# Softmax of a decoding kernel with paired heads: the subtraction of the maxima on GpSimd, one exponential for both batches, the sums on VectorE, and one copy for a transposed activation

## The chip, the cores and the metric

The kernel runs on one core of one Trainium2 chip. The metric is the device time of one execution in microseconds. A profiled execution also leaves a trace, from which the profile page and all rows below come. Its span runs from the first to the last instruction; the device time contains the span and a little around it.

## The reference

One decoding step of a transformer block, in float32, for a batch of 2 and one new token each: the normalized input goes through attention over the last 2048 positions of a cache (32 heads of 128) and, in parallel, through a bilinear gated layer; both are added to the input.

```python
B, Sq, D = 2, 1, 512            # Hq = Hkv = 32, Sk = 8192, Dh = 128, F = 1376
W = min(4096, max(256, Sk // 4))                     # 2048 positions
xn = _layernorm(x, axis=-1)
q = (xn @ wq).reshape(B, Sq, Hq, Dh).transpose(0, 2, 1, 3)
k, v = k_cache[:, :, Sk - W:, :], v_cache[:, :, Sk - W:, :]
p = softmax(einsum("bhqd,bhkd->bhqk", q, k) * Dh ** -0.5)
A = einsum("bhqk,bhkd->bhqd", p, v).transpose(0, 2, 1, 3).reshape(B, Sq, Hq * Dh) @ wo
h = (xn @ w_gate) * (xn @ w_up)
return x + A + h @ w_down
```

Nearly all the bytes are the keys and values: 2 batches x 32 heads x 2048 positions x 128 x 4 bytes, twice.

## The kernel before, in words

**The stream.** All inputs but a small tail are laid out in one array in the order in which they are used, and come in as large transfers, all issued by SyncE. `blocks()` writes that order out by hand: a small first load (`first`: the input, two selection matrices and a piece of wq), then loads of up to 31 blocks of 512 elements per partition (7936 KB), and smaller ones at the end. A field is the keys of a head (`k`, 8 blocks, both batches), its values (`v`, 8 blocks), a slice of wq (1 block), a slice of wo (1 block), or a piece of the gated layer's weights. The values run three heads behind the keys (`LAG = 3`). The `steps` pool has three buffers. `pump()` issues the next load as soon as one is free, and `done()` counts the fields of a buffer down and calls `pump()` when the last one was used. So a buffer is given back by VectorE (after the sums over a head's keys) or by TensorE (after the values and wo), whichever comes last.

**Order.** `InOrder` keeps the instructions of TensorE, VectorE, ScalarE and SyncE in program order; waits between engines come from the tiles that they share. GpSimd's instructions stand outside of it, on their own queue. `groups()` cuts the work by units (keys or values of a head): after the first heads, groups alternate between two heads of keys with one of values (keys 4 and 5 with values 1; 7 and 8 with 4; and so on) and one head of keys with two of values (6 with 2 and 3; 9 with 5 and 6). The main loop runs these groups through head 27 (`EARLY`); heads 28 to 31 are written out by hand behind it, with filler matmuls (`keep_busy`) in between.

**One head.** `products(h)` multiplies, in place, the keys by q (128 x 4096 elements on VectorE; q stands in PSUM, spread over all partitions by `project_q`). `sums(h)` reduces each product over the 128 elements of the head: 32 scores per partition, 16 for each batch. `maxima(h)` takes the maximum per partition on VectorE and across partitions on GpSimd (`mm`). `weights(h)` turns it into a negative bias on ScalarE (`nm`), and takes one exponential for each batch, 16 elements each, whose accumulated sums go to `rs`; GpSimd adds these across the partitions (`sum`), and `reciprocals(h)`, one head later, inverts them on VectorE (`rec`). The weights land in a ring of six tiles `p` which is zero elsewhere, in the columns that `side(h)` gives (1 for every third head, else 0); as TensorE's stationary operand a slice of 16 columns of it gives both batches and two sides their own rows of the result. `values` multiplies the values by them (`weigh`), copies the result out (ScalarE), transposes it (`transpose`), scales each column by `rec` into `oT` (ScalarE), and projects by wo into `acc`.

**The gate.** After head 3, `gate()` multiplies the two halves of the gated layer and transposes the product by matmuls into `tr`; after each of four of these ScalarE copies six columns into `hT`; pieces of the remainder go to `hX`. `down` then multiplies by w_down.

**The end.** The last weighings, projections and w_down pieces follow the last loads; two halves of the output are added up and stored by SyncE and ScalarE.

Of the kernel before, what the change touches and what calls it, by code (L numbers as in the profile page):

```python
# [8 lines left out]
F32 = mybir.dt.float32  # L9
AF = mybir.ActivationFunctionType  # L10
ALU = mybir.AluOpType
AX = mybir.AxisListType
# [4 lines left out]
P = 128  # L17
B, D, H, DH, SK, F = 2, 512, 32, 128, 8192, 1376
W = min(4096, max(256, SK // 4))
J = W // P  # L20
NC = D // P
FB = 4 * P
NFB = -(-F // FB)
# [10 lines left out]
JG = J // 4  # L34
# [10 lines left out]
OWN = 4  # L45
TG = [(0, 8, OWN), (8 * OWN, FT - 8 * OWN, 1)]
TP = FT
PADS = 480, 376


def k(h):
# [28 lines left out]
def groups():  # L80

    units = [u for h in range(LAG, H - 1) for u in (("k", h), ("v", h - LAG))]
    parts = [[("k", 0), ("k", 1)], [("k", 2)], units[:2]]
    parts += [units[i : i + 3] for i in range(2, len(units), 3)]
    return [[[i for kind, i in p if kind == want] for want in "kv"] for p in parts]
# [61 lines left out]
def kernel(  # L147
# [8 lines left out]
    nc = tc.nc  # L156
    pe, dve, act, sp = (InOrder(tc, e) for e in (nc.tensor, nc.vector, nc.scalar, nc.sync))
    SCALE = float(DH) ** -0.5
    BUFS = 3

    const = ctx.enter_context(tc.tile_pool(name="const", bufs=1))
    steps = ctx.enter_context(tc.tile_pool(name="steps", bufs=BUFS))
    small = ctx.enter_context(tc.tile_pool(name="small", bufs=6))
# [3 lines left out]

    const.tile([P, PADS[0]], F32, name="pad0")
    wd_tail = const.tile([TP, D], F32, name="wd_tail")

    todo, at = [], 0
# [31 lines left out]
    def done(kind, i):  # L203
        nonlocal held
        _, key = got.pop((kind, i))
        left[key] -= 1
        if left[key] == 0 and key[0] != "f":
            del tiles[key]
            held -= 1
            pump()  # L210
# [21 lines left out]
    o_ps = [ps_c.tile([P, 4 * DH], F32, name=f"o_ps{i}") for i in range(2)]  # L232
# [2 lines left out]
    gu_ps = o_ps  # L235

    NP = 6
    p_ring = [const.tile([P, B, JG, 8 * B], F32, name=f"p{i}") for i in range(NP)]
    for t in p_ring:
        nc.gpsimd.memset(t, 0.0)  # L240


    oT_ring = [const.tile([P, M], F32, name=f"oT{i}") for i in range(4)]
# [2 lines left out]
    tr = ps_c.tile([P, 4 * P], F32, name="tr")  # L246
# [20 lines left out]
        xnb, xn.rearrange("p c b -> p (c b)").unsqueeze(2).to_broadcast([P, NC * B, P])  # L267
    )

    q_ps, s_t, mm_t, p_t, sum_t, rec_t, oT = {}, {}, {}, {}, {}, {}, {}  # L270
    n_acc = bank = 0

    def side(h):

        return int(h % 3 == 0)
# [3 lines left out]
    def project_first(i):  # L279
        w = got["w", i][0].rearrange("p (c n) -> p c n", c=NC)  # L280
        if i == 0:
            q = q_first
        else:
            q_ps[0] = ps_q.tile([P, B, GC], F32, name="q")
            q = q_ps[0][:, :, DH:]
        for b in range(B):
            for c in range(NC):
                pe.matmul(
                    q[:, b, :], xnb[:, c * B + b, :], w[:, c, :],
                    start=(c == 0), stop=(c == NC - 1),  # L290
                )
        done("w", i)

    def project_q(h):

        if h + HG >= H:
            return
        g, c = h // HG + 1, h % HG
        if c == 0:
            q_ps[g] = ps_q.tile([P, B, GC], F32, name="q")  # L300
        for b in range(B):
            pe.matmul(
                q_ps[g][:, b, :], xnb[:, c * B + b, :], got["wq", h][0],
                start=(c == 0), stop=(c == NC - 1),
            )
        done("wq", h)

    def k_of(h):
        return got["k", h][0].rearrange("p (b j d) -> p b j d", b=B, j=J)

    def products(h):
        g, hh = divmod(h, HG)
        kt = k_of(h)
        qb = q_ps[g][:, :, hh * DH : (hh + 1) * DH] if h else q_first
        dve.tensor_tensor(
            kt, kt, qb.unsqueeze(2).to_broadcast([P, B, J, DH]), op=ALU.mult
        )

    def sums(h):
        s_t[h] = small.tile([P, B, J], F32, name="s")  # L320
        dve.tensor_reduce(s_t[h], k_of(h), axis=AX.X, op=ALU.add)
        done("k", h)

    def maxima(h):
        s = s_t[h]
        m = small.tile([P, B], F32, name="m")
        dve.tensor_reduce(m, s, axis=AX.X, op=ALU.max)
        mm = small.tile([P, B], F32, name="mm")
        nc.gpsimd.partition_all_reduce(mm, m, P, bass_isa.ReduceOp.max)  # L329
        mm_t[h] = mm  # L330

    def weights(h):
        s, mm = s_t.pop(h), mm_t.pop(h)
        nm = small.tile([P, B], F32, name="nm")
        act.mul(nm, mm, -SCALE)
        p_t[h] = p_ring[h % NP]
        rs = small.tile([P, B], F32, name="rs")
        for b in range(B):
            act.activation(
                p_t[h][:, b, :, 8 * side(h) + 4 * b : 8 * side(h) + 4 * b + 4],  # L340
                s[:, b, :].rearrange("p (i r) -> p i r", r=4),
                AF.Exp, bias=nm[:, b : b + 1], scale=SCALE, accum_out=rs[:, b : b + 1],
            )
        sum_t[h] = small.tile([P, B], F32, name="sum")
        nc.gpsimd.partition_all_reduce(sum_t[h], rs, P, bass_isa.ReduceOp.add)  # L345

    def reciprocals(h):
        rec_t[h] = small.tile([P, B], F32, name="rec")
        dve.reciprocal(rec_t[h], sum_t.pop(h))
# [13 lines left out]
    def weigh(h, v, parts, first, last):  # L363

        for n, part in enumerate(parts):
            b, i = divmod(part, JG)
            pe.matmul(
                o_ps[bank][32 * i : 32 * i + 8 * B, :], p_t[h][:, b, i, :],
                v[:, FB * n : FB * (n + 1)], start=first and b == 0, stop=last and b == B - 1,
            )  # L370

# [45 lines left out]
    def values(heads):  # L417
        transpose(heads, pv(heads))
        for h in heads:
            project_o(h)  # L420


    hT = const.tile([P, 4, NFB, M], F32, name="hT")
# [18 lines left out]
    def gate():  # L442
        g_sb = small.tile([P, FB], F32, name="o_sb", bufs=2)
        act.copy(g_sb, gu_ps[0])
        h_sb = small.tile([P, FB], F32, name="o_sb", bufs=2)
        dve.tensor_tensor(h_sb, g_sb, gu_ps[1], op=ALU.mult)
        for i in range(4):
            t = tr[:, P + i * P // 2 : P + i * P // 2 + NFB * B]
            pe.matmul(t, h_sb[:, i * P : (i + 1) * P], rows, start=True, stop=True)
            act.copy(hT[:, i, :, :], t.rearrange("p (n b) -> p n b", b=B))  # L450
        f = (NFC % 4) * P
        own = slice((NFB - 1) * B, NFB * B)
        for i in range(2):
            t = tr[HP * i : HP * i + RX, P + P // 4 : P + P // 4 + NFB * B]
            pe.matmul(t, h_sb[:, f - M : f + FX], rows, start=True, stop=True)
            act.copy(hX[HP * i : HP * i + RX, i, :], t[:, own])
            one = rows[HP * i : HP * i + M, 2 * i * B : 2 * i * B + B]
            act.copy(hX[HP * i : HP * i + M, i, :], one)
        f += FX
        t = tr[:TP, P + 3 * P // 4 : P + 3 * P // 4 + NFB * B]  # L460
        pe.matmul(t, h_sb[:, f : f + TP], rows, start=True, stop=True)
        act.copy(hX[:TP, 2, :], t[:, own])
# [35 lines left out]
    spare_in = xnb.rearrange("p a b -> p (a b)")  # L498
    for i in range(2):
        project_first(i)  # L500
    for ks, vs in groups()[:-2]:
        for n, h in enumerate(ks):
            products(h)
            project_q(h)
            if 2 <= h <= 3:
                project_gu(h - 2)
            sums(h)
            if h == LAG:
                gate()
            if vs and n == 0 and h < EARLY:  # L510
                values(vs)
            if h == LAG:
                down(0)
                down_rest()
            maxima(h)
            weights(h)
            if h >= 1:
                reciprocals(h - 1)
            if h == EARLY:
                values(vs)  # L520

# [2 lines left out]
        keep_busy(GC)  # L524
    for h in (H - 4, H - 3):
        products(h)
        if h == H - 3:
            for i, n in enumerate((FB, FB, FB, 448)):
                pe.matmul(
                    spare[:, :n], mean_w, got["k", h][0][:, i * FB : i * FB + n],  # L530
                    start=True, stop=True,
                )
        sums(h)
        maxima(h)
        weights(h)
        reciprocals(h - 1)

    h = H - 2
    products(h)
    sums(h)  # L540
    o_sbs = pv([H - 7]), pv([H - 6, H - 5])
    transpose([H - 7], o_sbs[0], 1 - bank)
    transpose([H - 6, H - 5], o_sbs[1])
    keep_busy(256)
    for i in range(H - 7, HF):
        project_o(i)
    maxima(h)
    reciprocals(h - 1)
    products(h + 1)
# [8 lines left out]
    accumulate(carry, acc_sb)  # L558
    project_o(HF)
    weights(h)  # L560

    keep_busy(GC)
# [23 lines left out]
    down(3)  # L586
    const.tile([P, PADS[1]], F32, name="pad1")
    acc_late = spare[:, :HP]
# [124 lines left out]
```

## Time and profile before

| | |
|---|---|
| time, median of 3 runs (lowest, highest) | 376.15 us (376.04, 376.19) |
| profiled execution | 376.13 us |
| its span | 374.5 us |
| mean granted TensorE clock | 0.831 |
| busy: TensorE, VectorE, ScalarE, GpSimd | 256.5, 294.7, 57.3, 25.2 us |
| read from memory | 159.47 MB, 426 GB/s over the span |

In rows of the trace, PE is TensorE (PEld its weight loads), DVE VectorE, ACT ScalarE, POOL GpSimd and SP SyncE; a letter q behind it is the engine's queue, which issues transfers. A row of a group names line, engine and operation, then out<-in by the program's tiles, the shapes, and how many; then busy us, mean ns of one, and the idle time of the engine before them with what ended it. A row of the timeline begins with the start and the length in us, and ends in brackets with the idle time before it. Most instructions carry line 131, which is the helper that keeps the order, so groups are told apart by their tiles: `s` are the scores, `m` and `mm` the maxima, `p` the weights, `step` the streamed buffers.

### The profile page before, as it was taken

What the parts mean: (1) busy time and instruction counts of PE and PEld (TensorE: products, weight loads), DVE (VectorE), ACT (ScalarE), POOL (GpSimd) and SP (SyncE); (2) the same over time, 40 slices, a digit from 0 to 9 for tenths busy, and PEclk for the clock granted to TensorE, in tenths of its full rate; (3) what the DMA queues carried; (4) which work ended last, traced back from release to release, by engine and by line L of the source; (5) the groups of instructions that cost most, each with busy time, mean ns of one, the idle gap of its engine ahead of it and who ended that gap; (6) DMA issues with size and microseconds to landing.
All of it is one profiled execution on the core that took longest, in us unless ns stands there. A gap on an engine that the chain in (4) does not pass through costs nothing.

```text
span 374.5 us, 2893 instructions
## 1 busy us (share of the span) xinstructions
PE 256.5 (68%) x1106; PEld 89.4 (24%) x1106; DVE 294.7 (79%) x145; ACT 57.3 (15%) x260; POOL 25.2 (7%) x74
## 2 busy tenths in 40 slices
PE   3166696884586861584958904896565857599897
PEld 3132123231222210121322202232111212133244
DVE  3069999369979559999359999894699999999760
ACT  1002011110211210020112001112010210112131
POOL 1000000000001000000100000010000000000010
PEclk9999696799576997598878875889666898689999
DMA  8999999999999999999999999999999999999996
GB/s 345 433 459 460 433 415 441 434 434 435 429 428 434 434 434 434 436 427 434 434 434 430 434 441 434 434 430 427 434 434 434 436 427 434 434 434 411 423 418 261
DMA packets 4232, 159.70 MB, mean 426 GB/s; under 512 B 730, under 2 KB 986, under 8 KB 1276
## 3 DMA queue, kind: packets, MB, share of 16 engines
q1 hardware_dynamic: 4076, 159.50, 98.7%
q8 instruction: 8, 0.13, 0.1%
q10 hardware_dynamic: 144, 0.03, 0.0%
q14 instruction: 4, 0.03, 0.0%
HBM read 159.47 MB, written 0.07 MB: 426 GB/s over the span
## 4 chain that ended last, share of the span: by engine, by line
DMA 66%; PE 17%; DVE 14%; ACT 1%; issue 1%; SPq 0%; DVEq 0%
DMA step<-in_stream_dram 66%; DVE s L131 7%; DVE step L131 7%; PE q L131 6%; PE o_ps L131 6%; PE acc L131 4%; PE tr L131 2%; ACT o_sb L131 1%; ACT oT L131 0%; DVE m L131 0%; SPq L131 0%; DVE o_out L131 0%; DVE rec L131 0%; DVEq L131 0%
## 5 line engine op out<-in xcount | busy, mean ns | idle before, releaser
L131 DVE TENSOR_TENSOR step<-step,q 128x4096 f32<-128x4096 f32 x31 | 136.8, 4412 | 45.0 <-DMA step<-in_stream_dram 41.4
L131 DVE TENSOR_REDUCE s<-step 128x32 f32<-128x4096 f32 x32 | 141.4, 4419 | 1.1
L131 PE MATMUL o_ps<-step,p 128*16 128x512 f32 x512 | 75.9, 658 | 47.3 <-DMA step<-in_stream_dram 47.3
L131 PE MATMUL q<-step,xnb 128*128 128x512 f32 (+1 forms) x128 | 76.9, 748 | 32.3 <-DMA step<-in_stream_dram 32.3
L131 PEld LDWEIGHTS q<-step,xnb 128*128 128x128 f32 x128 | 28.9, 242 | 83.2 <-issue 66.8
L131 PE MATMUL acc<-step,oT 128*2 128x512 f32 (+1 forms) x88 | 36.6, 576 | 8.6 <-ACT oT L131 8.6
L131 PE MATMUL tr<-first,o_sb 128*128 128x2 f32 (+4 forms) x190 | 29.6, 274 | 15.8 <-ACT o_sb L131 11.9
L131 PEld LDWEIGHTS o_ps<-step,p 128*16 128x16 f32 x512 | 13.7, 100 | 100.1 <-DMA step<-in_stream_dram 56.9
L131 PEld LDWEIGHTS tr<-first,o_sb 128*128 128x128 f32 (+2 forms) x190 | 27.0, 217 | 39.4 <-ACT o_sb L131 33.4
L131 ACT COPY o_sb<-o_ps 128x512 f32<-128x512 f32 x23 | 13.5, 586 | 145.5 <-PE o_ps L131 145.3
L329 POOL PARTITION_ALL_REDUCE mm<-m x32 | 11.4, 357 | 242.6 <-DVE rec L131 136.6
L131 ACT ACTIVATE nm<-mm 128x2 f32<-128x2 f32 x32 | 6.6, 206 | 128.8 <-POOL mm L329 128.8
L131 ACT ACTIVATE p<-s,nm 128x16 f32<-128x16 f32 x64 | 19.2, 300 | 1.0
L345 POOL PARTITION_ALL_REDUCE sum<-rs x32 | 12.7, 398 | 95.8 <-ACT p L131 95.8
L131 PE MATMUL o_ps<-step,xn 128*2 128x512 f32 (+1 forms) x48 | 14.6, 670 | 6.2 <-DMA step<-in_stream_dram 6.2
L131 ACT ACTIVATE oT<-tr,rec 128x1 f32<-128x1 f32 x64 | 12.1, 260 | 27.7 <-PE tr L131 27.7
L131 DVE TENSOR_TENSOR step<-step,tr 128x4096 f32<-128x4096 f32 x1 | 4.4, 4420 | 15.1 <-DMA step<-in_stream_dram 15.1
L131 ACT ACTIVATION_READ_ACCUMULATOR p<-s,nm 128x1 f32 x64 | 11.9, 187 | 0.0
L131 PE MATMUL q<-xnb,mean_w 128*128 128x512 f32 (+5 forms) x26 | 10.1, 496 | 0.0
L131 PEld LDWEIGHTS acc<-step,oT 128*2 128x2 f32 x88 | 4.2, 87 | 21.0 <-ACT oT L131 12.1
L131 DVE RECIPROCAL rec<-sum 128x2 f32<-128x2 f32 x32 | 5.0, 155 | 4.0 <-POOL sum L345 4.0
L131 PEld LDWEIGHTS o_ps<-step,xn 128*2 128x2 f32 x48 | 2.9, 95 | 17.9 <-issue 10.9
(45 smaller groups left out, 48.3 us busy)
## 6 DMA issues: line engine op xcount, KB each, us to landing
step<-in_stream_dram SPq DMA_DIRECT2D x15, 7936.0 KB, 35.0
step<-in_stream_dram SPq DMA_DIRECT2D x1, 7808.0 KB, 38.8
step<-in_stream_dram SPq DMA_DIRECT2D x1, 7680.0 KB, 20.9
step<-in_stream_dram SPq DMA_DIRECT2D x1, 7552.0 KB, 57.2
step<-in_stream_dram SPq DMA_DIRECT2D x1, 4864.0 KB
step<-in_stream_dram SPq DMA_DIRECT2D x1, 3328.0 KB, 19.6
step<-in_stream_dram SPq DMA_DIRECT2D x1, 2048.0 KB, 24.1
step<-in_stream_dram SPq DMA_DIRECT2D x1, 1280.0 KB, 19.0
```

Source lines behind the costliest of these rows:

```text
L131: made = call(*args, **kwargs)
L329: nc.gpsimd.partition_all_reduce(mm, m, P, bass_isa.ReduceOp.max)
L345: nc.gpsimd.partition_all_reduce(sum_t[h], rs, P, bass_isa.ReduceOp.add)
```

## The change

The main loop handles the two heads of a two-head group together where both have the same side, which is so for all pairs from 4 and 5 on; heads 0 to 3 and the groups of one head stay single. Heads 28 to 31 keep the old form of the weights.

- The scores of a pair stand in one tile. `maxima` takes one maximum and one reduction across partitions for the pair.
- `weights_of` subtracts the maxima on GpSimd and takes one exponential for both batches and all heads of the group, without bias and without accumulated sums.
- `denominators` sums the weights on VectorE and adds them across partitions on GpSimd. It is called for the group before the present one, behind the present group's exponential. `reciprocals_of` inverts them after the first product of the group after that.
- The six tiles of weights become four, holding one, two, one and two heads. Eight columns of room per head are added, so that the two batches and the columns of `side` lie at even steps. The first pad shrinks by 48 elements, by which the rings grow.
- In `gate()` the four transposes write next to each other and one copy moves all of `hT`.

```diff
-PADS = 480, 376
+PADS = 432, 376
...
-    p_ring = [const.tile([P, B, JG, 8 * B], F32, name=f"p{i}") for i in range(NP)]
+    PW = B * JG * 8 * B
+    p_ring = [const.tile([P, 1 + i % 2, PW + 4 * B], F32, name=f"p{i}") for i in range(4)]
...
+    def p_at(heads):
+        n, at = divmod(heads[0] % NP, 3)
+        at = max(at - 1, 0), 2 * n + min(at, 1)
+        return p_ring[at[1]][:, at[0] : at[0] + len(heads), :]
+
+    def p_of(heads):
+        c = 8 * side(heads[0])
+        t = p_at(heads).rearrange("p h (b x) -> p h b x", b=B)
+        t = t[:, :, :, : PW // B].rearrange("p h b (i y) -> p h b i y", i=JG)
+        return t[:, :, :, :, c : c + 4]
...
+    def maxima(*heads):
+        n = len(heads)
+        m = small.tile([P, 2, B], F32, name="m", bufs=4)[:, :n]
+        dve.tensor_reduce(m, s_t[heads], axis=AX.X, op=ALU.max)
+        mm = small.tile([P, 2, B], F32, name="mm")[:, :n]
+        flat = [t.rearrange("p h b -> p (h b)") for t in (mm, m)]
+        nc.gpsimd.partition_all_reduce(*flat, P, bass_isa.ReduceOp.max)
+        mm_t[heads] = mm
+
+    def weights_of(heads):
+        s, mm = s_t.pop(heads), mm_t.pop(heads)
+        n = len(heads)
+        e = small.tile([P, 2, B, J], F32, name="e", bufs=2)[:, :n]
+        nc.gpsimd.tensor_tensor(
+            e, s, mm.unsqueeze(3).to_broadcast([P, n, B, J]), op=ALU.subtract
+        )
+        act.activation(
+            p_of(heads), e.rearrange("p h b (i r) -> p h b i r", r=4), AF.Exp, scale=SCALE
+        )
+
+    def denominators(heads):
+        n = len(heads)
+        rs = small.tile([P, 2, B], F32, name="rs")[:, :n]
+        dve.tensor_reduce(rs, p_of(heads), axis=AX.XY, op=ALU.add)
+        t = small.tile([P, 2, B], F32, name="sum")[:, :n]
+        flat = [t.rearrange("p h b -> p (h b)") for t in (t, rs)]
+        nc.gpsimd.partition_all_reduce(*flat, P, bass_isa.ReduceOp.add)
+        sum_t[heads] = t
+
+    def reciprocals_of(heads):
+        rec = small.tile([P, 2, B], F32, name="rec")[:, : len(heads)]
+        dve.reciprocal(rec, sum_t.pop(heads))
...
         for i in range(4):
-            t = tr[:, P + i * P // 2 : P + i * P // 2 + NFB * B]
+            t = tr[:, P + i * NFB * B : P + (i + 1) * NFB * B]
             pe.matmul(t, h_sb[:, i * P : (i + 1) * P], rows, start=True, stop=True)
-            act.copy(hT[:, i, :, :], t.rearrange("p (n b) -> p n b", b=B))
+        t = tr[:, P : P + 4 * NFB * B].rearrange("p (i n b) -> p i n b", i=4, b=B)
+        act.copy(hT, t)
...
+    last = ready = None
     for ks, vs in groups()[:-2]:
         for n, h in enumerate(ks):
+            heads = tuple(ks) if len({side(i) for i in ks}) == 1 else (h,)
             products(h)
+            if ready:
+                reciprocals_of(ready)
+                ready = None
             project_q(h)
...
-            sums(h)
+            sums(h, heads)
...
-            maxima(h)
-            weights(h)
-            if h >= 1:
-                reciprocals(h - 1)
+            if h == heads[-1]:
+                maxima(*heads)
+                weights_of(heads)
+                if last:
+                    denominators(last)
+                last, ready = heads, last
...
     for h in (H - 4, H - 3):
         products(h)
+        reciprocals_of(ready)
...
-        reciprocals(h - 1)
+        if h == H - 4:
+            denominators(last)
+            ready = last
+    reciprocals(H - 4)
```

More of the change, by code (lines that the diff above doesn't have):

```diff
@@ L268 @@
     )
-    q_ps, s_t, mm_t, p_t, sum_t, rec_t, oT = {}, {}, {}, {}, {}, {}, {}
+    q_ps, s_t, mm_t, sum_t, rec_t, oT = {}, {}, {}, {}, {}, {}
     n_acc = bank = 0
@@ L317, in products, with sums @@
         )
-    def sums(h):
-        s_t[h] = small.tile([P, B, J], F32, name="s")
+    def sums(h, heads=None):
+        heads = heads or (h,)
+        if h == heads[0]:
+            s = small.tile([P, 2, B, J], F32, name="s", bufs=2)
+            for n, i in enumerate(heads):
+                s_t[i] = s[:, n]
+            s_t[heads] = s[:, : len(heads)]
         dve.tensor_reduce(s_t[h], k_of(h), axis=AX.X, op=ALU.add)
         done("k", h)
[L324 to L330, printed above, removed]
+    def maxima(*heads):
[6 more added lines that the diff above has]
+        mm_t[heads] = mm
@@ L332, in weights @@
+    def reciprocals_of(heads):
+        rec = small.tile([P, 2, B], F32, name="rec")[:, : len(heads)]
+        dve.reciprocal(rec, sum_t.pop(heads))
+        for n, h in enumerate(heads):
+            rec_t[h] = rec[:, n]
     def weights(h):
-        s, mm = s_t.pop(h), mm_t.pop(h)
-        nm = small.tile([P, B], F32, name="nm")
+        s, mm = s_t.pop(h), mm_t.pop((h,))[:, 0]
+        nm = small.tile([P, B], F32, name="nm", bufs=2)
         act.mul(nm, mm, -SCALE)
-        p_t[h] = p_ring[h % NP]
@@ L339, in weights @@
             act.activation(
-                p_t[h][:, b, :, 8 * side(h) + 4 * b : 8 * side(h) + 4 * b + 4],
-                s[:, b, :].rearrange("p (i r) -> p i r", r=4),
+                p_of((h,))[:, 0, b], s[:, b, :].rearrange("p (i r) -> p i r", r=4),
                 AF.Exp, bias=nm[:, b : b + 1], scale=SCALE, accum_out=rs[:, b : b + 1],
@@ L367, in weigh @@
             pe.matmul(
-                o_ps[bank][32 * i : 32 * i + 8 * B, :], p_t[h][:, b, i, :],
+                o_ps[bank][32 * i : 32 * i + 8 * B, :],
+                p_at((h,))[:, 0, 8 * B * part : 8 * B * (part + 1)],
                 v[:, FB * n : FB * (n + 1)], start=first and b == 0, stop=last and b == B - 1,
```

## The prediction

> **What bounds the kernel now.** I read the page first (busy shares, chain, transfers), then the windows cut at the arrivals of loads, then the chain in order of time, then VectorE's own timeline. From the page:
>
> ```profile
> span 374.5 us, 2893 instructions
> ...
> PE 256.5 (68%) x1106; PEld 89.4 (24%) x1106; DVE 294.7 (79%) x145; ACT 57.3 (15%) x260; POOL 25.2 (7%) x74
> ...
> DMA 66%; PE 17%; DVE 14%; ACT 1%; issue 1%; SPq 0%; DVEq 0%
> ...
> step<-in_stream_dram SPq DMA_DIRECT2D x15, 7936.0 KB, 35.0
> ...
> step<-in_stream_dram SPq DMA_DIRECT2D x1, 3328.0 KB, 19.6
> ```
>
> No compute engine is full: VectorE has 79%, and ScalarE and GpSimd, from which the change takes and to which it gives, have 15% and 7%. The chain that ended last is mostly transfer. The windows say how steady that transfer is (core line: stretch, its length, busy time of each engine, granted clock, DMA share, GB/s):
>
> ```profile
> 40.49:59.30 18.81, 16.84 (x54) 3.85 (x54) 18.31 (x9) 2.46 (x12) 1.70 (x5) 0.86 0.97 418
> 59.30:78.30 19.00, 16.41 (x64) 5.69 (x68) 9.19 (x4) 3.19 (x17) 0.73 (x2) 0.73 0.99 428
> ...
> 97.03:360.03 263.00, 184.50 (x732) 60.27 (x732) 225.11 (x99) 41.97 (x197) 18.48 (x50) 0.80 1.00 433
> ...
> 371.00:374.50 3.50, 1.67 (x72) 1.05 (x61) 0.45 (x2) 0.61 (x4) 0.00 (x0) 1.00 0.17 49
> ```
>
> For 263 us the DMA engines are full (share 1.00) at 433 GB/s while the other engines come and go, and the bytes end near 371 us. One load of 7936 KB is 8.13 MB, which at 433 GB/s takes 18.8 us; its median landing is 35.0 us after its issue, so it is issued some 16 us before its turn. The queue only runs dry if a buffer comes free later than that. The pieces of the chain give the tightest places:
>
> ```profile
> 159.93 31.07 DMA step<-in_stream_dram
> ...
> 360.08 1.91 PE o_ps L131 x16
> ...
> 372.74 0.22 DVE o_out L131
> ```
>
> The load issued at 159.93 lands 31.07 us later: 12.3 us ahead of its turn. The 3328 KB load (3.41 MB, 7.9 us) lands in 19.6: 11.8 us ahead. An early one is closest:
>
> ```profile
> 49.16 0.36 SPq L131 DMA_DIRECT2D step<-in_stream_dram  x1
> ...
> 78.36 4.42 DVE L131 TENSOR_TENSOR step<-step,q 128x4096 f32<-128x4096 f32 x1 [7.90 <-DMA step<-in_stream_dram]
> ```
>
> Issued at 49.16 and awaited by VectorE until 78.3: 29.1 less 18.8 is 10.3 us ahead. So anything that makes a buffer come free up to 10 us later changes no arrival. From 360 on, TensorE's last weighings and projections follow the last arrivals closely and end in the output add at 372.74.
>
> VectorE gives the buffers back; how much it may lose is in its waits and its timeline:
>
> ```profile
> DVE step L131 <- DMA step<-in_stream_dram: 56.5, 16, 15.1
> ...
> 134.92 4.42 DVE L131 TENSOR_TENSOR step<-step,q 128x4096 f32<-128x4096 f32 x1 [8.23 <-DMA step<-in_stream_dram]
> ...
> 191.09 4.42 DVE L131 TENSOR_TENSOR step<-step,q 128x4096 f32<-128x4096 f32 x1 [9.61 <-DMA step<-in_stream_dram]
> ...
> 209.70 4.42 DVE L131 TENSOR_TENSOR step<-step,q 128x4096 f32<-128x4096 f32 x1 [0.38 <-DMA step<-in_stream_dram]
> ...
> 340.70 4.42 DVE L131 TENSOR_TENSOR step<-step,q 128x4096 f32<-128x4096 f32 x1 [0.42 <-DMA step<-in_stream_dram]
> ...
> 352.25 4.42 DVE L131 TENSOR_TENSOR step<-step,q 128x4096 f32<-128x4096 f32 x1 [2.39 <-DMA step<-in_stream_dram]
> ```
>
> It waits 56.5 us in all for loads, 41.4 of it after the first 15.1, in long waits (8.23, 9.61) and short ones (0.38, 0.42).
>
> **The change part by part.** In the main loop 28 heads become 20 groups: 8 pairs (4 and 5, 7 and 8, up to 25 and 26) and 12 single heads. The last four heads keep the old form. Durations (forms kept apart; busy us, mean ns):
>
> ```profile
> L131 DVE TENSOR_REDUCE s<-step 128x32 f32<-128x4096 f32 x32 | 141.4, 4419 | 1.1
> ...
> L131 ACT ACTIVATE p<-s,nm 128x16 f32<-128x16 f32 x64 | 19.2, 300 | 1.0
> ...
> L345 POOL PARTITION_ALL_REDUCE sum<-rs x32 | 12.7, 398 | 95.8 <-ACT p L131 95.8
> ...
> L131 ACT ACTIVATION_READ_ACCUMULATOR p<-s,nm 128x1 f32 x64 | 11.9, 187 | 0.0
> L329 POOL PARTITION_ALL_REDUCE mm<-m x32 | 11.4, 357 | 242.6 <-DVE rec L131 136.6 <-DVE m L131 105.9
> L131 ACT ACTIVATE nm<-mm 128x2 f32<-128x2 f32 x32 | 6.6, 206 | 128.8 <-POOL mm L329 128.8
> ...
> L131 DVE TENSOR_REDUCE m<-s 128x2 f32<-128x32 f32 x32 | 5.9, 186 | 1.1
> ...
> L131 DVE RECIPROCAL rec<-sum 128x2 f32<-128x2 f32 x32 | 5.0, 155 | 4.0 <-POOL sum L345 4.0
> ...
> L240 POOL MEMSET p<- 128x128 f32 x6 | 0.9, 204 | 0.3 <-POOLq L690 0.3
> ...
> L131 ACT COPY hT<-tr 128x6 f32<-128x6 f32 x4 | 0.7, 164 | 5.9 <-PE tr L131 5.9
> ```
>
> *ScalarE.* Removed: 28 heads times (0.206 + 2 x 0.300 + 2 x 0.187) = 28 x 1.18 = 33 us. Added: 20 exponentials over 32 or 64 elements, which I take at the 0.30 of the row for 16, so 6 us. Busy falls from 57 to about 30. Worth on the path: nothing, since ScalarE is 1% of the chain and mostly waits. If one exponential cost 1 us instead, 14 us would still fit.
>
> *GpSimd subtract.* No row shows one. Low end 0.15 (six fills of 128x128 in 0.91 us, pipelined); high end 4.42, if it had to stand aside for one large VectorE instruction. I take 0.35, the cross-partition reduction, the nearest row that reads and writes small tiles on GpSimd. It stands between the two cross-partition reductions in GpSimd's queue, so the three take 0.36 + 0.35 + 0.40 = 1.1 us (0.9 to 5.2). Behind them on GpSimd is nothing else; waiting for them are the exponential and, at the next group, VectorE's reciprocal. That reciprocal stands behind a product of 4.42 us, so at 1.1 us it never waits; at 5.2 it waits 0.8 us in each of about 19 groups, 15 us, under 41.4. Cost: 0 at both ends. What the trace has on blocking:
>
> ```profile
> 31.15 4.41 DVE L131 TENSOR_TENSOR step<-step,q 128x4096 f32<-128x4096 f32 x1
> 31.32 0.35 POOL L329 PARTITION_ALL_REDUCE mm<-m  x1 [29.70 <-DVE m L131]
> ```
>
> A GpSimd instruction starts and ends inside a VectorE product at its usual 0.35 us, which speaks for the low end. The Trainium skill, "SBUF — State Buffer", section "SBUF: two separate sides", warns that VectorE and GpSimd share a pair of ports under an exclusive lock, the loser blocking for the whole instruction; VectorE takes it in a two-port mode or, against a GpSimd reader, with two SBUF inputs. By that rule the products (one input from SBUF, q from PSUM) and the sums (one input) take no lock and the subtract waits for nothing; read as a lock for every VectorE instruction it gives the 5.2 us, and the sum is the same by both. The trace agrees with the first reading, and the rule makes the rival on GpSimd below less likely, not more.
>
> *VectorE.* Start to start the small instructions cost less than they last:
>
> ```profile
> 117.38 0.19 DVE L131 TENSOR_REDUCE m<-s 128x2 f32<-128x32 f32 x1
> 117.48 0.15 DVE L131 RECIPROCAL rec<-sum 128x2 f32<-128x2 f32 x1
> 117.55 4.40 DVE L131 TENSOR_TENSOR step<-step,q 128x4096 f32<-128x4096 f32 x1
> ```
>
> 0.10 us for the maximum, 0.07 for the reciprocal. The sum of weights reads as many elements as the maximum: 0.10. A pair reads 32 elements more; from 186 ns for 32 and 4419 for 4096 that is 0.03. Single group: +0.10 (12 times, 1.2 us). Pair: 0.13 + 0.13 + 0.07 against 2 x 0.17, no change. Together +1.2 us over the span, at most 0.2 us between two long waits, inside even the waits of 0.38 and 0.42. Near the end (heads 28 and 29) there are two small instructions more, about 0.2 us, ahead of the product at 340.70 with its 0.42, and 2.39 more before 352.25. Bounds in time: 0 to 0.
>
> *Later weights and reciprocals.* The first head of a pair gets its weights one head (9.1 us) later, and denominators come two groups behind. Values run three heads behind, so the pair 7, 8 has its weights near 119 us and TensorE needs them only with the load before 134.92: cover 16 us. The reciprocals are closer. ScalarE's scaled copies that read them:
>
> ```profile
> 138.62 0.41 ACT L131 ACTIVATE oT<-tr,rec 128x1 f32<-128x1 f32 x2 [1.14 <-PE tr L131]
> ...
> 194.69 0.72 ACT L131 ACTIVATE oT<-tr,rec 128x1 f32<-128x1 f32 x4 [1.96 <-PE tr L131]
> ```
>
> Head 7's reciprocal now follows the product of head 10, which ends at 139.34, so this copy moves to about 139.5, 0.9 us later; head 12's follows that of head 15 (ends 195.51), 0.6 us later. Queued behind it: ScalarE's later exponential (not yet due), TensorE's output projection and through it a buffer's release, which has 10 us or more. Cost 0; without that cover it would be 0.9.
>
> *hT in one copy.* Three copies of 0.164 and three hand-overs between TensorE and ScalarE go:
>
> ```profile
> 58.79 0.39 PE L131 MATMUL tr<-first,o_sb 128*128 128x6 f32 x2 [1.84 <-DVE o_sb L131]
> ...
> 61.86 0.38 PE L131 MATMUL tr<-first,o_sb 128*64 128x6 f32 x2 [0.25 <-ACT hT L131]
> ```
>
> The second row is the first instruction after the four transposes, so these take 3.1 us from start to start, and need about 4 x 0.4 plus one copy of 0.2 without the hand-overs: TensorE gains 1.3 us at 60 us. The next loads are already queued, so the gain ends in a longer wait for the load of 78.3: worth 0. If no load stood queued, the 1.3 us would be the most it could bring.
>
> *Layout.* The rings take 48 elements more, the first pad 48 less, so the streaming buffers stay put and only the tiles ahead of the rings move by 192 bytes, the first small load among them:
>
> ```profile
> first<-in_stream_dram SPq DMA_DIRECT2D x1, 271.0 KB, 2.8
> ```
>
> Its 0.28 MB are 0.64 us at 433 GB/s. Half speed would cost 0.6, double speed save 0.3; I take 0, as 0.64 is too little to show either.
>
> Sum: 0 + 0 + 0 + 0 + 0 against the profiled execution's 376.13 (span 374.5 and 1.6 around it), which stands 0.02 below the median of 376.15. **Predicted: 376.1 us.** This measurement can tell 0.2%, 0.75 us, from no change.
>
> **The rivals.**
> *A, faster: the early stretch fills up.* Between 40.49 and 78.30 the transfers ran at 418 and 428 GB/s, not 433: 18.81 x 15/433 + 19.00 x 5/433 = 0.87 us. If shorter hand-overs at the gate or fewer ScalarE instructions let the DMA engines reach 433 there, the time is 375.3; with the saved 0.3 of the first load, 375.0. Against it: two loads stand queued there already, so nothing of the compute feeds that rate.
>
> *B, slower: GpSimd becomes the pace.* Place: subtract between the reductions, then the reciprocal on VectorE. If the three exceed a product's 4.42 us, VectorE waits the excess per group. It decides once 19 x (X - 4.42) exceeds 41.4 plus the 10 us of early issue, X = 7.1 us. With the subtract held for a whole product and sum (8.84), X is 9.6: 98 - 51 = 47 us, so 423 us. For it: no row of a subtract. Against it: the reduction inside a product above, and needing 6 us for 64 elements. The Trainium skill, "GPSIMD Engine Reference", section "2.1 Instruction dispatch", says that the first call of a freshly loaded routine pays about 6 us of code loading; were that paid at each change between reduction and subtract, X would be about 13 by its figure, an estimate, but the trace's first reduction at 31.32 took 0.35 like all the others, and one payment would vanish in the early waits.
>
> *C, slower: the end is disturbed.* Place: heads 28 to 31 on VectorE. Spare there is 0.42 + 2.39 = 2.8 us; a late reciprocal that costs a whole product's 4.42 would pass on 1.6: 377.7. Against it: GpSimd's three would have to take 5 us more.
>
> *D, slower: the moved first tile,* half speed: 376.7, still within 0.2%; a little beyond with a late start of the first statistics.
>
> **How the numbers follow.** Everything hidden: 0.80. A: 0.07. B: 0.04. C: 0.05. D: 0.04, half of it within 0.2%. So faster 0.07, same 0.82, slower 0.11. The range takes in A without its extra (375.3) and D with the 0.2 of VectorE's small instructions (376.9): 375.3 to 376.9.
>
> **What would show it.** ScalarE near 30 us; 20 subtracts on GpSimd of 0.15 to 0.5 us; VectorE near 296 with some 55 us of waits for loads; the large loads' median landing still about 35 us; 433 GB/s between 97 and 360 us; the copies at 138.62 and 194.69 under a microsecond later; the end at 372 to 373. I am wrong if a window of the middle falls below 430 GB/s (a dry queue), if reciprocals wait for GpSimd by microseconds, if the last arrival moves, or if the early stretch reaches 433.

## The result, and the profile after

The changed kernel takes 540.4 us (median of 6 runs, 536.2 to 544.3) where the kernel before took 376.0 in the runs beside it: a ratio of 1.434 (95% interval 1.430 to 1.439). One of the six runs, over 1.5% above the fastest, is left out of the ratio. The forecast of no change was wrong by 164 us.

The page of the changed kernel, with the lines that answer to those of before:

```profile
span 534.3 us, 2827 instructions
...
PE 259.0 (48%) x1106; PEld 98.2 (18%) x1106; DVE 294.1 (55%) x149; ACT 36.0 (7%) x137; POOL 24.8 (5%) x76
...
DMA  9999889489968771933959296986952914990392
GB/s 389 445 424 431 333 380 428 181 339 424 428 272 366 304 304 39 418 153 133 399 229 447 86 447 238 452 329 285 380 228 76 448 86 162 447 373 0 121 420 114
...
issue 49%; DVE 33%; PE 9%; DMA 4%; POOL 3%; ACT 1%; POOLq 0%; SPq 0%; DVEq 0%
...
step<-in_stream_dram SPq DMA_DIRECT2D x15, 7936.0 KB, 22.0
```

VectorE, ScalarE and GpSimd are busy for as long as before or less. TensorE's 1106 matmuls take 259.0 us against 256.5, at a granted clock of 0.709 against 0.831. The loads now run dry again and again (slices of 0, 39 and 76 GB/s), and a large load lands 22.0 us after its issue, hardly more than its own 18.8: buffers come back too late to queue it early. The chain has turned round, from 66% transfer to 4%. Its largest part, 49%, is "issue": an engine that waits for nothing the profile shows. The waits say which engine:

```profile
POOL e L355 <- issue: 194.4, 20, 11.9
...
DVE rec L131 <- POOL sum L368: 161.1, 14, 26.2
POOL mm L348 <- issue: 123.8, 14, 11.3
...
POOL sum L368 <- issue: 43.4, 5, 11.1
...
DVE rs L131 <- ACT p L131: 38.1, 9, 6.6
...
DVE step L131 <- DMA step<-in_stream_dram: 15.5, 1, 15.5
```

(Waiter, what it waited for, us in total, times, the longest.) GpSimd stands idle 361.6 us in 39 waits for "issue", 9.3 us each. VectorE waits for GpSimd's sums and, through ScalarE's exponential, for its subtracts; it no longer waits for a load after the first one. GpSimd's timeline shows where its idle lies:

```profile
175.96 0.37 POOL L348 PARTITION_ALL_REDUCE mm<-m  x1 [10.11 <-issue]
185.98 0.23 POOL L355 TENSOR_TENSOR e<-s,mm 128x32 f32<-128x32 f32 x1 [9.64 <-issue]
196.44 0.44 POOL L368 PARTITION_ALL_REDUCE sum<-rs  x1 [10.23 <-issue]
210.53 0.38 POOL L348 PARTITION_ALL_REDUCE mm<-m  x1 [13.65 <-DVE rs L131]
210.82 0.48 POOL L368 PARTITION_ALL_REDUCE sum<-rs  x1
```

The subtract lasts 0.23 us. But 9 to 10 us pass before it, and as many before the reduction behind it. Between two reductions in a row (the last two rows) nothing passes. So it is the change of kind that costs, reduction to subtract and back. The built program's list of GpSimd instructions shows what stands at these places, one instruction without operands ahead of each change:

```
27 L355 ISA
28 L355 TENSOR_TENSOR e<-s,mm 128x32
29 L348 ISA
30 L348 ISA mm<-m 128x4
31 L368 ISA sum<-rs 128x2
32 L355 ISA
33 L355 TENSOR_TENSOR e<-s,mm 128x64
```

The program names it PseudoReloadLibraryIndex. It holds 41 of them here, one for each of the 40 changes and one ahead of the first reduction, and 1 in the kernel before. The stored trace has each as two records named MODIFY_POOL_CONFIG, which the views leave out: behind the subtract of 185.98 they start at 186.41 and 186.45 and take 0.001 us each, and the reduction starts at 196.44. So the price counts as no busy time and stands in the profile as idle for "issue".

### The profile page after: what moved, and what is told of

Its sections match the earlier page's. It is cut to its first block, busy times and chain, and to the rows that moved or that the text cites. A ratio compares the mean times of both kernels' runs of the same rounds, so it can differ in the third digit from the quotient of the medians.

```text
span 534.3 us, 2827 instructions
## 1 busy us (share of the span) xinstructions
PE 259.0 (48%) x1106; PEld 98.2 (18%) x1106; DVE 294.1 (55%) x149; ACT 36.0 (7%) x137; POOL 24.8 (5%) x76
## 4 chain that ended last, share of the span: by engine, by line
issue 49%; DVE 33%; PE 9%; DMA 4%; POOL 3%; ACT 1%; POOLq 0%; SPq 0%; DVEq 0%
DVE step L131 18%; DVE s L131 14%; DMA step<-in_stream_dram 4%; PE o_ps L131 3%; PE q L131 2%; PE tr L131 2%; PE acc L131 2%; POOL sum L368 1%; POOL mm L348 1%; POOL e L355 1%; DVE rs L131 0%; ACT o_sb L131 0%; ACT p L131 0%; DVE m L131 0%; DVE rec L131 0%
## 5 line engine op out<-in xcount | busy, mean ns | idle before, releaser
L131 PE MATMUL tr<-first,o_sb 128*128 128x2 f32 (+4 forms) x190 | 38.3, 323 | 201.2 <-ACT o_sb L131 170.4
L131 DVE RECIPROCAL rec<-sum 128x2 f32<-128x2 f32 (+1 forms) x24 | 4.0, 167 | 163.5 <-POOL sum L368 161.1
L131 PE MATMUL q<-step,xnb 128*128 128x512 f32 (+1 forms) x128 | 73.6, 722 | 18.4 <-DMA step<-in_stream_dram 11.7
L131 PEld LDWEIGHTS tr<-first,o_sb 128*128 128x128 f32 (+2 forms) x190 | 36.1, 283 | 220.9 <-ACT o_sb L131 188.3
L131 PE MATMUL acc<-step,oT 128*2 128x512 f32 (+1 forms) x88 | 48.1, 715 | 42.0 <-ACT oT L131 42.0
L131 PE MATMUL o_ps<-step,p 128*16 128x512 f32 x512 | 63.7, 624 | 0.0
L131 ACT ACTIVATE p<-e 128x32 f32<-128x32 f32 (+1 forms) x20 | 4.8, 240 | 387.5 <-POOL e L355 387.5
L131 DVE TENSOR_REDUCE rs<-p 128x2 f32<-128x32 f32 (+1 forms) x20 | 3.9, 194 | 38.1 <-ACT p L131 38.1
L355 POOL TENSOR_TENSOR e<-s,mm 128x32 f32<-128x32 f32 (+1 forms) x20 | 5.0, 251 | 194.4 <-issue 194.4
L131 PE MATMUL acc<-step,hT 128*2 128x128 f32 (+2 forms) x56 | 6.7, 331 | 0.0
```

The costliest lines, as they stand in the source:

```text
L131: made = call(*args, **kwargs)
L355: nc.gpsimd.tensor_tensor(e, s, mm.unsqueeze(3).to_broadcast([P, n, B, J]), op=ALU.subtract)
```

## The experiments

Theory K is that price of a change of kind. Against it stood L (the later weights and reciprocals of the new order stall the engines), P (VectorE's large instructions hold GpSimd's subtract off), and S or E (each subtract costs a fixed share on the path). The first four runs tell these apart.

**The subtract on VectorE, all else as changed** (e1).

```diff
-        nc.gpsimd.tensor_tensor(
+        dve.tensor_tensor(
             e, s, mm.unsqueeze(3).to_broadcast([P, n, B, J]), op=ALU.subtract
```

> The changed kernel, with the subtraction of the maxima alone moved from GpSimd to VectorE. Theory K (a change of kind on GpSimd, from reduction across partitions to subtract and back, costs 6 to 12 us each time, and GpSimd becomes the pace): no change of kind is left, so 376 us, within 0.2% of the kernel before; VectorE busy some 4 us more and about 0.45 us of wait for the maximum in each of 20 groups, under its idle. Rival L (the later weights and reciprocals of the new order are what stalls VectorE and TensorE): they stay, so still 500 us or more.

Measured: 376.29 us against 375.94, ratio 1.0003 (0.9992 to 1.0013). The page, and a window of this run:

```profile
PE 258.8 (69%) x1106; PEld 90.4 (24%) x1106; DVE 297.6 (79%) x169; ACT 37.3 (10%) x137; POOL 20.0 (5%) x56
...
97.03:360.03 263.00, 184.72 (x732) 60.12 (x732) 227.24 (x118) 26.46 (x102) 14.61 (x37) 0.79 1.00 433
```

The stream is full again. One instruction's engine is the whole loss, and the rest of the change, taken together (paired heads, one exponential, later denominators, one copy of hT, moved tiles) is worth nothing either way. L falls.

**An unread subtract in the kernel before** (e2).

```diff
         mm_t[h] = mm
+        if h <= EARLY and not (h >= 4 and h % 3 == 1):
+            e = small.tile([P, B, J], F32, name="e", bufs=2)
+            nc.gpsimd.tensor_tensor(
+                e, s, mm.unsqueeze(2).to_broadcast([P, B, J]), op=ALU.subtract
+            )
```

(The second pad is smaller by the size of the new tile.)

> The kernel before, with one GpSimd subtract more in 20 of the first 28 heads (the heads that end a group in the changed kernel); nobody reads its result. Theory K: each such head has two changes of kind on GpSimd, some 10 us each, between the maximum and the sum of its weights, so GpSimd needs about 21 us for a marked head and 20 x 21 = 420 us in the loop: 470 to 560 us in all. Rival L: nothing waits for the subtract and the order is the old one, so 376 us. Rival P (GpSimd's subtract is held off by VectorE's large instructions through a shared port): at most 4.4 us per subtract, off the path, 376 to 380 us.

Measured: 549.6 us, one run. Its waits:

```profile
DVE rec L131 <- POOL sum L350: 218.9, 21, 14.8
POOL e L333 <- issue: 202.9, 20, 12.2
...
POOL sum L350 <- issue: 175.3, 20, 11.5
```

A result that nobody reads slows the old kernel by 174 us, through the reduction queued behind it and VectorE's reciprocal behind that. P and L both foretold 376 to 380.

**GpSimd alone** (e3). The body is replaced by this pair (shortened) in a loop, without stream, beside it, and beside VectorE:

```python
nc.gpsimd.partition_all_reduce(mm, m, P, bass_isa.ReduceOp.max)
nc.gpsimd.tensor_tensor(e, s, mm, op=ALU.subtract)   # m of the next is taken from e
```

> GpSimd alone: reductions across partitions and subtracts of the same size in turn, each reading the other's result; 6 pairs with nothing else running, 8 pairs beside nine loads of 7936 KB, 4 pairs beside VectorE products and sums of 128x4096. No attention is computed. Theory K: idle of about 6 us before every instruction in the quiet part and beside VectorE, 9 to 12 us beside the loads. Rival P: no idle in the quiet part and beside the loads, up to 4.4 us beside VectorE.

Rows of GpSimd's timeline: three with nothing else running, two beside the loads, two beside VectorE's products and sums; ahead of them the page's row of transfers in 40 slices of 8 us:

```profile
GB/s 4 0 0 0 0 0 0 0 0 0 355 402 449 402 409 449 394 465 394 465 386 433 433 394 465 378 465 386 488 394 433 145 95 0 0 0 0 0 0 0
...
6.88 0.37 POOL L172 PARTITION_ALL_REDUCE mm<-m  x1 [6.45 <-issue]
14.81 0.23 POOL L174 TENSOR_TENSOR e<-s,mm 128x32 f32<-128x32 f32 x1 [7.56 <-issue]
21.01 0.37 POOL L172 PARTITION_ALL_REDUCE mm<-e  x1 [5.97 <-issue]
...
102.93 0.23 POOL L174 TENSOR_TENSOR e<-s,mm 128x32 f32<-128x32 f32 x1 [10.81 <-issue]
114.16 0.37 POOL L172 PARTITION_ALL_REDUCE mm<-e  x1 [11.00 <-issue]
...
277.60 0.23 POOL L174 TENSOR_TENSOR e<-s,mm 128x32 f32<-128x32 f32 x1 [6.84 <-issue]
283.66 0.37 POOL L172 PARTITION_ALL_REDUCE mm<-e  x1 [5.83 <-issue]
```

This is the price itself. After the first two, a change costs 5.8 to 6.9 us in quiet (to the reduction about 5.9, to the subtract about 6.8), the same beside VectorE (5.8 to 7.1), and 9.5 to 12.9 us while loads run. P falls. The first reduction of a run pays too (6.45). The quiet changes leave no trace among the transfers (0 GB/s), so how the loads lengthen them isn't shown. The Trainium skill, "GPSIMD Engine Reference", section "2.1 Instruction dispatch", gives approximately 6 us for loading the code of a freshly loaded routine, without a visible instruction; the quiet price agrees, the price beside loads is nearly double its figure, and here it is paid at each change and not once.

**The subtract twice in a row** (e5): `weights_of` issues it a second time into a tile of its own.

> The changed kernel, with the GpSimd subtract issued twice in a row, the second into a tile that nobody reads. Theory K: the second is of the kind already there and costs its 0.25 us, 20 x 0.25 = 5 us: 540 to 550 us. Rival P, or a fixed start-up cost of some 10 us for any GpSimd subtract: 20 x 4.4 to 20 x 10 us more, 620 us or over.

Measured: 539.7 us, one run, at the lower end of K's 540 to 550. GpSimd's timeline:

```profile
106.44 0.23 POOL L355 TENSOR_TENSOR e<-s,mm 128x32 f32<-128x32 f32 x1 [10.33 <-issue]
106.64 0.23 POOL L359 TENSOR_TENSOR e<-s,mm 128x32 f32<-128x32 f32 x1
112.58 0.39 POOL L348 PARTITION_ALL_REDUCE mm<-m  x1 [5.71 <-issue]
```

The second starts 0.2 us behind the first. Subtracts are cheap, changes are not.

**One kind of work in the loop** (e6). TensorE takes the reductions, and GpSimd keeps its 20 subtracts:

```diff
+    def means(*heads):
...
+        d = tr[:, 16 : 16 + n * B]
+        pe.matmul(d, mean_w, flat[1], start=True, stop=True)
+        act.activation(flat[0], d, AF.Copy, scale=float(D // P))
...
-        nc.gpsimd.partition_all_reduce(*flat, P, bass_isa.ReduceOp.add)
...
+        t = tr[:, 20 : 20 + n * B]
+        pe.matmul(t, ones_w, rs.rearrange("p h b -> p (h b)"), start=True, stop=True)
...
-                maxima(*heads)
+                means(*heads)
```

> The changed kernel with its GpSimd subtract, but in the main loop the reductions across partitions are done by TensorE: a matmul with constant weights gives the mean over partitions of the maxima (any offset common to a softmax is as good) and the sum of the weights. GpSimd then does one kind of work until head 27 and changes once, before the last heads. Theory K: no change of kind, so 376 to 380 us with all 20 subtracts in place, no idle ahead of them but that for their input. Rival P (the subtract itself is slow or held off): 500 us or more.

Measured: 381.6 us, ratio 1.015 (1.014 to 1.017), a little above K's 376 to 380. The first row is from its waits, the others from VectorE's timeline:

```profile
POOL e L368 <- ACT mm L131: 302.8, 19, 31.5
...
322.20 4.42 DVE L131 TENSOR_TENSOR step<-step,q 128x4096 f32<-128x4096 f32 x1 [0.35 <-DMA step<-in_stream_dram]
...
332.19 0.18 DVE L131 RECIPROCAL rec<-tr 128x4 f32<-128x4 f32 x1 [5.58 <-ACT oT L131]
```

The subtracts are all there and wait for their input alone; 159 of the 164 us are gone. The 5.5 us left arise late. At 322.20 VectorE is 0.15 us behind the kernel before, which starts this product at 322.05. Then it waits 5.58 us, where little idle follows, for a reciprocal whose tile in PSUM TensorE and ScalarE still use.

**The same with the subtract on VectorE** (e11).

> The kernel with TensorE's reductions, and the subtract on VectorE as well, so that GpSimd has no work in the main loop. That kernel took 381.6 us, and its VectorE waits 5.6 us near the end for a reciprocal that follows TensorE and ScalarE. If that wait is the 5.5 us, moving the subtract changes nothing: 381 to 382 us. If the GpSimd subtract costs the 5.5 us (20 x 0.28 us), 376 us.

Measured: 395.2 us, one run, outside both expectations. Its waits:

```profile
DVE e L131 <- ACT mm L131: 57.4, 20, 13.3
...
DVE rec L131 <- ACT oT L131: 5.2, 1, 5.2
```

VectorE now waits 57.4 us for maxima that come by way of TensorE's and ScalarE's queues, a wait that GpSimd had borne without harm. The late wait for the reciprocal is still there, 5.2 us, with no subtract on GpSimd, so the subtract is not its cause. A smaller cost of the subtract in e6 can't be read from this run, which loses 19 us for another reason.

**How many changes can be hidden.** The next four ask how much of the price the kernel can take.

Pairs alone on GpSimd, the single heads subtracted by ScalarE (e4):

```diff
+        if n == 2:
             nc.gpsimd.tensor_tensor(
...
+        else:
+            nm = small.tile([P, B], F32, name="nm", bufs=2)
+            act.mul(nm, mm[:, 0], -1.0)
+            for b in range(B):
+                act.activation(
+                    e[:, 0, b, :], s[:, 0, b, :], AF.Identity, bias=nm[:, b : b + 1]
+                )
```

> The changed kernel, with the GpSimd subtract kept for the 8 pairs alone; for the 12 single heads ScalarE subtracts with a bias. 16 changes of kind are left of 40. Theory K with GpSimd as the pace: two changes at about 11 us and the small work make 23 us for a pair and the single head behind it, for which the loads take 32.6 us, so GpSimd is no longer the pace; VectorE still waits some 9 us per pair (2 for the exponential, 7 for the reciprocal), of which some 5 are its idle and 10 in all the early issue of loads: 376 to 400 us. Rival S (each subtract stands on the path and costs its share, (540 - 376)/20 = 8 us): 376 + 8 x 8 = 440 us.

Measured: 416.8 us, one run, between the two expectations. The unread subtract of e2 in four heads only (e7, `h in (8, 14, 20, 26)`), and in the early or the late two of them (e9, e10):

> The kernel before, with the unread GpSimd subtract in 4 heads only (8, 14, 20, 26): 8 changes of kind. Theory K with the cover that the prediction named (VectorE's idle and loads issued some 10 us early): each time VectorE waits some 12 us for a reciprocal, and about 10 us of idle lie between two of them, so the rest is taken by the early issue: 376 to 378 us. Without such cover, at the 8.7 us per marked head of the kernel with 20 of them ((549.6 - 376)/20): 376 + 35 = 411 us.

Measured: 395.1 us, ratio 1.048 (1.044 to 1.052), far above the 376 to 378 of the first account and below the 411 of no cover at all.

> The kernel before with the unread GpSimd subtract in heads 8 and 14 only. Theory V (what a change of kind costs is VectorE's wait for the reciprocal less the idle that VectorE still had ahead of it; loads issued early do not help): in the run with four such heads these two waits were 12.7 and 4.1 us, and VectorE's waits for loads behind head 8 sum to 25.6 us in the kernel before, so 376.0 us, no change. Rival E (each marked head costs its share, (395 - 376)/4 = 4.8 us): 385.5 us.

Measured: 378.6 us, ratio 1.007 (1.005 to 1.009).

> The kernel before with the unread GpSimd subtract in heads 20 and 26 only. Theory V: two waits of about 12 us each, 24 us, against 13 us that VectorE idles for loads and for TensorE behind head 20 (8.6, 0.6, 0.4, 0.6, 0.4, 2.4): 376 + 11 = 387 us. Rival E: 385.5 us as with the early two. The cover that the prediction counted (10 us of early issue beside the idle): 377 us. The two runs together tell V from E.

Measured: 390.9 us, ratio 1.041 (1.036 to 1.046). VectorE's timeline, of e9 (three rows) and of e10 (two):

```profile
139.14 0.17 DVE L131 RECIPROCAL rec<-sum 128x2 f32<-128x2 f32 x1 [13.89 <-POOL sum L350]
...
206.40 0.17 DVE L131 RECIPROCAL rec<-sum 128x2 f32<-128x2 f32 x1 [4.78 <-POOL sum L350]
...
268.02 4.42 DVE L131 TENSOR_TENSOR step<-step,q 128x4096 f32<-128x4096 f32 x1 [7.08 <-DMA step<-in_stream_dram]
```

```profile
270.69 0.17 DVE L131 RECIPROCAL rec<-sum 128x2 f32<-128x2 f32 x1 [13.54 <-POOL sum L350]
...
337.70 0.17 DVE L131 RECIPROCAL rec<-sum 128x2 f32<-128x2 f32 x1 [12.54 <-POOL sum L350]
```

The same number of changes costs 2.6 us early and 15 late, so a fixed price per subtract (S and E) falls. Theory V, with 376.0 and 387 us, comes nearest, but is low by 2.6 and 3.9. An early stall takes the place of waits for loads, or VectorE works its arrears off in those that follow (8.23, 9.61 and 8.61 us in the kernel before); behind the stall of 337.70 only 0.42 and 2.39 us of them are left. e9's 2.6 us are not stall: the load that VectorE gets at 265.83 in the kernel before arrives at 268.02, although the DMA engines are full (share 1.00 at 429 GB/s from 154 to 268 us). What slowed the stream there stays open.

The kernel before idles 49.0 us on VectorE between the first load and the end of head 31 (41.4 for loads, 3.6 for TensorE, 4.0 for sums). Against that stand the same waits in the other runs (rec: of the reciprocals, rs: of the sums of weights, gate: of the gated product, acc: of the copy out of `acc`):

| kernel | VectorE waits there, us | less 49.0 | span above 374.5 |
|---|---|---|---|
| changed | 163.5 (rec) + 38.1 (rs) + 5.8 (gate) + 2.5 (acc) = 209.9 | 160.9 | 159.8 |
| pairs alone (e4) | 50.7 (rec) + 28.7 (rs) + 10.4 (loads) + 1.2 (acc) = 91.0 | 42.0 | 40.7 |
| late two (e10) | 29.9 (rec) + 29.2 (loads) + 3.4 (TensorE) + 1.8 (acc) = 64.3 | 15.3 | 14.9 |
| early two (e9) | 22.4 (rec) + 28.3 (loads) + 1.0 (TensorE) = 51.7 | 2.7 | 2.2 |

VectorE's work hardly differs, so its waits must give the span; what the table adds is that waits for GpSimd first eat the waits for loads, and only the rest is lost.

**The copy of hT alone** (e8): the three lines of `gate()`, in the kernel before.

> The kernel before with the gate's transposes copied out in one copy, and nothing else of the change. The prediction's value: 376.0 us, no change within 0.2%, TensorE ready about 1.3 us earlier near 62 us and waiting that much longer. The prediction's rival A (the early stretch fills up): 375.0 to 375.3 us.

Measured: 376.03 us against 376.04, ratio 1.0001 (0.9992 to 1.0010). TensorE's timeline:

```profile
58.70 1.70 PE L131 MATMUL tr<-first,o_sb 128*128 128x6 f32 x8 [2.12 <-DVE o_sb L131]
60.66 0.38 PE L131 MATMUL tr<-first,o_sb 128*64 128x6 f32 x2 [0.27 <-ACT hT L131]
```

The remainder starts at 60.66 and not at 61.86: 1.2 us earlier, and worth nothing.

No version here beats the kernel before: with the stream full at 433 GB/s, work taken off the other engines brought nothing (e1, e8).

## Why the prediction was wrong

- **The step that failed** is the GpSimd subtract, "the three take 0.36 + 0.35 + 0.40 = 1.1 us (0.9 to 5.2)". The durations were right: the groups of the changed kernel give 0.23 and 0.28 for the subtract.

```profile
L355 POOL TENSOR_TENSOR e<-s,mm 128x32 f32<-128x32 f32 x12 | 2.8, 229 | 116.6 <-issue 116.6
...
L355 POOL TENSOR_TENSOR e<-s,mm 128x64 f32<-128x64 f32 x8 | 2.3, 282 | 77.8 <-issue 77.8
```

  But the time stands in the right-hand column, ahead of the instruction. From maximum to sum it was 20.9 us (175.96 to 196.88), four times the upper bound: two changes of kind of some 10 us each, a term that the sum did not have. The bound was taken from durations of other instructions, and the one change of kind in the trace of before, from the fills of `p` to the first reduction, has no price in any row.
- **Rival B named the mechanism and was set aside on a misread row.** "The trace's first reduction at 31.32 took 0.35 like all the others" looks for the price in the duration. It lies in the idle ahead, and that reduction had 29.70 us of idle: the records of its reload stand at 1.64 us. e3's first reduction shows 6.45. A chance of 0.04 was far too small for a price that no row bounded. Its threshold, 7.1 us, was passed threefold, and its worked time of 423 us was too low. Its formula was wrong too: with 20.9 us it gives 638 us, as it counts 16.5 us of wait in each of 19 groups, and the 160 us lost are 8.4 a group.
- **The cover was counted twice**, in "41.4 plus the 10 us of early issue": a load issued early keeps the stream full, but it doesn't let VectorE catch up. By e9 and e10 the idle that follows a stall is what counts. With this error e4 was expected at 376 to 400 us and came out at 416.8, e7 at 376 to 378 and came out at 395.
- **"Behind them on GpSimd is nothing else"** held only within a group. The maximum of the next group stands behind the change back, and e2 shows that a queue pays even for a result that nobody reads.
- **ScalarE**: 36.0 us busy, 30 foretold. The removed work was added up from durations that overlap; one old softmax took 0.93 us from start to end in the timeline and not 1.18, and 57.3 - 28 x 0.93 + 4.8 (20 exponentials of 0.24) is 36.1.
- **Right**: that the stream bounds the kernel before, and that all the rest costs nothing. The single exponential, the sums on VectorE, the later weights and reciprocals and the moved tiles, with the subtract on VectorE, are e1's ratio of 1.0003; hT's 1.3 us were 1.2 and hidden.
- **The lock on the ports** by the Trainium skill's "SBUF — State Buffer", section "SBUF: two separate sides", did not act: in e3 the subtract lasts 0.23 us and its change 6.7 to 7.1 us beside VectorE's products and sums, as in quiet, which agrees with the reading taken. It was rightly weighed and was the wrong danger.

## What to carry to other kernels

Before an operation is given to an engine that does another kind of work, look for a row in which that engine changes between the two; if there is none, the price of the change isn't bounded, and the chance of a loss must be large. On GpSimd keep one kind of work per phase, and put a lone elementwise step on an engine that is already there: here 0.2 us on VectorE, after some 0.55 us of wait for the maximum, against some 20 us. A stall is paid for by the idle that the stalled engine still has, so late stalls cost more (15 us of two waits of 13.54 and 12.54 in e10).

## What the runs showed of the hardware that was not expected

- A change between a reduction across partitions and an elementwise subtract on GpSimd costs 5.8 to 7.1 us each way in quiet or beside VectorE, and 9.5 to 12.9 us beside loads. It shows as idle, mostly for "issue", never as a busy instruction.
- Within the changed kernel too the price goes with the transfers. The first change below ran beside loads (409 GB/s from 123.4 to 133.5 us), the second in a gap of the stream (3 GB/s from 270.4 to 276.0 us):

```profile
133.59 0.37 POOL L348 PARTITION_ALL_REDUCE mm<-m  x1 [10.53 <-issue]
...
276.02 0.37 POOL L348 PARTITION_ALL_REDUCE mm<-m  x1 [5.96 <-issue]
```

- The change starts behind the last instruction of the old kind and does not wait for the next one's input. In e6 its records stand at 323.07 us, and the reduction that follows waits for VectorE until 337.05. So a change is hidden where GpSimd's next input comes late enough.
- The loads' own rate was lowered by it little, if at all: 433 GB/s between 90 and 140 us of e3 and 420 in the next 100 us; the kernel before has 435 from 97 to 247 us.

```profile
90.00:140.00 50.00, 0.00 (x0) 1.58 (x5) 1.00 1.02 433
```
